# Building the sink values of a new sequence one operation per step, over six steps

## The chip, the cores and the metric
The kernel runs on one core of one Trainium2 chip. The metric is the device time of one execution in microseconds, taken as the median over several executions. The profile is one execution recorded by the hardware profiler; its times are microseconds from the first instruction of the core.

## The reference, cut to what matters
Windowed attention with a few "sink" keys that every query may see, and behind it a dense layer with a softplus in the middle:
```
B, H, S, D = 4, 8, 768, 64          n_sink, window = 4, 128
scores = (1/sqrt(D)) * q @ k.T
keep   = (pos_k < n_sink) | ((pos_q - pos_k >= 0) & (pos_q - pos_k < window))
a      = softmax(where(keep, scores, -1e9))
x      = (a @ v) with the heads side by side            # [B*S, 512]
h      = x @ w_in                                       # w_in  [512, 2048]
out    = (max(h, 0) + log1p(exp(-abs(h)))) @ w_out      # w_out [2048, 512]
```

## The kernel before, in words
**Tiles.** The 4 sequences of 768 positions are cut into chunks of 256 positions, three to a sequence and twelve in all (chunks 0 to 11). A chunk has 8 heads. Chunks 0, 3, 6 and 9 are the first of their sequence. Chunks 0 and 1 (`EXACT = 2`) use full-precision operands; from chunk 2 on every matmul operand is split into a rounded high part and a remainder, and the matmuls run over both.

**Steps.** The work is a software pipeline with one step per head: step i = 8k + h. The first 17 steps are written out by hand in a string (`START`). From step 17 on a loop (L630 to L641) runs the same list of parts in each step: first the letters `JjGL`, then those of `STEADY`. A letter is a stage of some head ahead of or behind step i: `L` and `G` load, `p` and `q` split the loaded tiles, `S` the score matmuls, `T` the softmax, `N` the normalisation, `W` transposes the weights of head i and masks them, `V` the matmul of weights and values for head i, `O` its output, and `U F P R D E` are the dense layer of the chunk before. Each engine executes its instructions in the order in which this list issues them, and waits for data through semaphores. SyncE (SP) issues the loads and the stores in the same order.

**What GpSimd (POOL) does in a steady step**, in this order: the masking of the transposed weights into the tile `pt` (`W`, four selects, L308 and L311), in odd steps the remainder of the value tile `vv` (`q`, L56), the copy `gh` of the dense layer (`P`, L52), in odd steps the remainder `xl` (`O`, L56), and two normalisations of `a` (`N`, L264).

**What TensorE (PE) does in a steady step** that bears on the change: stage `V` (`values`, L316) first multiplies the sink weights with the sink values, `x<-sk,vs` (L327), and then the tile `pt` with the value tile, `x<-pt,vv` (L333); the other matmuls of the step are those of `h` (L459), `acc` (L496 to L498), the scores (L230, L231) and the transposes.

**The sink values.** `vs` is a tile of 128 partitions for a group of four heads, two groups (g = 0 and 1) to a sequence. Its lower 64 partitions hold the values of the sink keys of the group, each in the partition rows of its own head and zero elsewhere (a product with the 0/1 tile `hmask`, `_place`, L159): the left half of the columns holds the high part, the right half the remainder. Its upper 64 partitions are zero (`_zero`, L60). A new sequence is prepared as follows (k is its first chunk):
- step 8k-2, at its head (letter `J`): the load `vsr` of the raw values (L137, a DMA of SP), then on POOL the rounded copy `vsh` (L151), the remainder written back into `vsr` (L152), the zeroing of `vs` of group 0 (L154) and the two `_place` of group 0;
- step 8k+1, at its head (letter `j`): the zeroing and the two `_place` of group 1.

Heads 0 to 3 read group 0 in stage `V` of steps 8k to 8k+3, heads 4 to 7 group 1 in steps 8k+4 to 8k+7. The tiles have one buffer each (`bufs=1`). In the steady loop this happens for k = 3, 6 and 9, around steps 24, 48 and 72. The same for sequence 0 happens once in exact form and once more for chunk 2, whose `J` and `j` stand at steps 14 and 17.

Of the kernel before, what the change touches and what calls it, by code (L numbers as in the profile page):

```python
# [11 lines left out]
F32 = mybir.dt.float32  # L12
F32R = mybir.dt.float32r
# [7 lines left out]
B, H, S, D = 4, 8, 768, 64  # L21
DM, DFF = 512, 2048
P = 128
# [4 lines left out]
CT = CH * P  # L28
# [8 lines left out]
BIG = 3.0e38  # L37
G = 4
ORDERED = {mybir.EngineType.PE, mybir.EngineType.SP}


class Ctx:
# [16 lines left out]
def _zero(nc, out, finite):  # L59
    nc.gpsimd.tensor_scalar(out, finite, 0.0, 0.0, ALU.mult, ALU.add)  # L60
# [62 lines left out]
class _Attention:  # L123
# [16 lines left out]
    def sinks(self, g):  # L140

        c, nc, b = self.c, self.c.nc, self.b
        raw = c.vsr[b]
        if self.exact:
            c.vs[b, g] = c.lp.tile([P, G, D], F32, tag=f"vsf{g}", name=f"vsf{g}", bufs=1)
            nc.gpsimd.memset(c.vs[b, g][:], 0.0)
            self._place(c.vs[b, g][:32], raw[:32, g : g + 1], 32)
            return
        if g == 0:
            c.vsh[b] = c.lp.tile([64, 2, D], F32R, tag="vsh", name=f"vsh{b}", bufs=1)  # L150
            nc.gpsimd.tensor_scalar(c.vsh[b][:], raw[:], 1.0, 0.0, ALU.mult, ALU.add)  # L151
            nc.gpsimd.tensor_tensor(raw[:], raw[:], c.vsh[b][:], ALU.subtract)  # L152
        c.vs[b, g] = c.lp.tile([P, G, P], F32R, tag=f"vs{g}", name=f"vs{b}_{g}", bufs=1)
        _zero(nc, c.vs[b, g][64:].rearrange("p (a e) d -> p a (e d)", a=2), c.sk[64:].bitcast(F32).unsqueeze(1).broadcast_to([64, 2, CT]))  # L154
        for src, o in ((c.vsh[b], 0), (raw, D)):
            self._place(c.vs[b, g][:64, :, o : o + D], src[:, g : g + 1], 64)

    def _place(self, out, src, rows):
        self.c.nc.gpsimd.tensor_tensor(  # L159
# [350 lines left out]
def _fast(c):  # L510
# [5 lines left out]
    n = c.nchunks  # L516
    att = [_Attention(c, k) for k in range(n)]
# [24 lines left out]
    def stage(kind):  # L542
        def run(i):
            if not todo[kind]:
                return
            o, e = todo[kind][0]
            before = "acdl"["acdl".index(kind) - 1]
            while kind != "a" and todo[before] and todo[before][0][0] <= o:
                stage(before)(i)
            home = _turn(c.WM, o)  # L550
            if kind == "a":
                while any(u is c.upper[c.turn] for u in c.top.values()):
                    stage("c")(i)
            elif kind == "c" and home == "p":
                while sum(_turn(c.WM, k) == "p" for k, _ in todo["l"] if k < o) > 1:
                    stage("l")(i)
            todo[kind].pop(0)
            if kind == "a":
                _weight_top(c, e, _turn(c.WT, o))
            elif kind == "c":  # L560
                _weight_f32(c, e, home)
            elif kind == "d":
                _weight_high(c, e, engine(c.WH, o))
            else:
                _weight_low(c, e, _turn(c.WL, o) if home == "s" else "V")

        return run
# [11 lines left out]
    def sinks(g):  # L579
        def run(i):  # L580
            k = (i - g * G) // H
            if (i - g * G) % H == 0 and k < n and (att[k].first or k == c.EXACT):
                if g == 0 and k:
                    att[k].load_sinks()
                att[k].sinks(g)

        return run

    parts = {
        "S": (call(att, "scores"), G),  # L590
# [15 lines left out]
        "G": (call(att, "load_v", 2), 2),  # L606
        "L": (call(att, "load"), G + 2),
        "J": (sinks(0), 2),
        "j": (sinks(1), G - 1),
        "w": (dma, 0),  # L610
        **{kind: (stage(kind), 0) for kind in "acdl"},
    }
# [183 lines left out]
def _kernel(tc, a, out):  # L796
# [7 lines left out]
    with ExitStack() as keep:  # L804
        c.const = keep.enter_context(tc.tile_pool(name="const", bufs=1))
        c.wp = keep.enter_context(tc.tile_pool(name="wp", bufs=1))
        c.w, c.raw, c.top, c.word = {}, {}, {}, {}
        c.ident = c.const.tile([P, P], F32, name="ident")
        c.stats = c.const.tile([P, B * H * NB], F32, name="stats")
        c.room = c.const.tile([P, 2, 4 * FP], F32, name="room")  # L810
        nc.gpsimd.memset(c.room[:], 1.0)
        c.sk = c.const.tile([P, CT], F32R, name="sk")
        ones = c.room[:].rearrange("p a b -> p (a b)").unsqueeze(1).broadcast_to([P, CT // 64, 64])
        _zero(nc, c.sk[:].rearrange("p (a b) -> p a b", b=64), ones)
        with ExitStack() as st:
            pool = lambda n, bufs: st.enter_context(tc.tile_pool(name=n, bufs=bufs))
            psum = lambda n, bufs: st.enter_context(tc.tile_pool(name=n, bufs=bufs, space=bass.MemoryType.PSUM))
            c.xp, c.mp, c.stg = pool("xp", 2), pool("mp", 2), pool("stg", 4)
            c.lp, c.ap, c.sp = pool("lp", 2), pool("ap", 2), pool("sp", 2)
            c.ps_acc, c.ps_h = psum("ps_acc", 1), psum("ps_h", 2)  # L820
            c.ps_s, c.ps_t, c.ps_x = psum("ps_s", 2), psum("ps_t", 1), psum("ps_x", 1)
            with tc.manual_schedule(engines=ORDERED):
                _fast(c)
        ok = nc.values_load(c.flag[:1, :1], min_val=0, max_val=1)
        with tc.If(ok < 1):
            _general(c)
# [8 lines left out]
Ctx.WT = "PAAVVVVAVAAVAAAVAAAAAAAAAAAPAAAV"  # L835
Ctx.WH = "VAPAAVAAAAVPPAAAAVVAVAAAAAVAVAAA"
Ctx.WL = "PPPPPPPVPPVPPVPPVPVPPPPVVPVVPVPV"
Ctx.STEADY = ("kWUqpKSFTRDVPONE", "SWTkpUKERDNFPqVO")
Ctx.START = """
S0 G4 T0 w w S1 j4 T1 J0 w L8 w w S3 S2 N0 N1 T2 W0 L10 w N2 S4 T3 N3 a w T4 k0 a c K0 a S5 c W1 w w  # L840
d S6 V0 O0 l d V1 w c l T5 N4 W2 T6 d w a S7 c O1 W3 l N5 G6 N6 a T7 c V2 N7 a d S8 k4 a O2 W4 w T8
# [62 lines left out]
```

## Time and profile before
| | |
|---|---|
| median of 3 runs | 740.09 us |
| lowest and highest run | 737.24 and 740.62 us |
| span of the profiled execution | 735.7 us, 13883 instructions |
| mean granted TensorE clock of that execution | 0.986 of full |
| busy: PE, DVE, ACT, POOL | 95%, 75%, 61%, 54% of the span |

The page of the profile gives the span of the profiled execution, from its first to its last instruction, and no other time of its own for it; the median of the runs lies 4.4 us above this span and the lowest run 1.5 us above it. A row of a timeline gives the start in us, the duration in us, the engine, the line, the operation, the output and input tiles with their shapes, how many instructions were merged, and in square brackets the idle time of the engine just before with the instruction that ended it. A row of the waits names who waited for whom, then the total in us, the number of times and the longest. A row of the table of windows gives the stretch, its length, the busy time and instruction count of PE, PEld (the weight loads), DVE, ACT and POOL, and then the granted clock, the DMA share and GB/s.

### The profile page before, as it was taken

The numbers are of one execution on the slowest core, as the hardware profiler recorded it, in microseconds if no ns is written. First come the engines' busy times: TensorE is split into PE (matmuls) and PEld (weight loads), VectorE is DVE, ScalarE is ACT, GpSimd is POOL, SyncE is SP. The second block draws the span as 40 slices with busy tenths as digits, with TensorE's granted clock in tenths as the row PEclk, the third lists the DMA queues.
The fourth block names the chain that finished last, engine by engine and source line by source line (L and its number), as shares of the span: only waits on it lengthen the run. The fifth ranks groups of instructions, "written<-read, shape, count | busy, mean of one in ns | idle before, by whom it ended". The sixth has DMA issues, their size and how long they took to land.

```text
span 735.7 us, 13883 instructions
## 1 busy us (share of the span) xinstructions
PE 699.7 (95%) x4489; PEld 624.8 (85%) x4489; DVE 552.6 (75%) x1608; ACT 446.1 (61%) x1098; POOL 400.7 (54%) x773
## 2 busy tenths in 40 slices
PE   4788899989999999998999999998999999999996
PEld 3567688979899999997899999997999999999995
DVE  5899997867877877876977887886887877754331
ACT  3577865655666666665666666665766756644331
POOL 4866476565555665665655655556655565553110
PEclk9899999999999999999999999999999999999999
DMA  8877611411321321321321322322222222100001
GB/s 291 310 255 235 187 40 48 126 46 44 98 67 49 105 61 54 93 63 42 92 74 49 95 69 57 95 60 61 62 74 77 83 61 76 58 13 0 30 1 35
DMA packets 40876, 63.22 MB, mean 86 GB/s; under 512 B 4634, under 2 KB 22362, under 8 KB 40794
## 3 DMA queue, kind: packets, MB, share of 16 engines
q1 hardware_dynamic: 36042, 45.47, 21.2%
q10 hardware_dynamic: 4752, 16.77, 6.5%
q8 instruction: 38, 0.62, 0.4%
q14 instruction: 44, 0.36, 0.2%
HBM read 55.93 MB, written 6.29 MB: 85 GB/s over the span
## 4 chain that ended last, share of the span: by engine, by line
PE 83%; DVE 6%; POOL 4%; ACT 3%; DMA 1%; issue 1%; ACTq 0%; SPq 0%; POOLq 0%; DVEq 0%
PE h L459 34%; PE acc L496 11%; PE acc L498 11%; PE acc L497 11%; PE x L333 6%; PE t L297 2%; PE s L230 2%; PE s L231 2%; PE x L327 2%; PE s L227 1%; ACT a L250 1%; POOL a L264 1%; DMA wo71r<-w 1%; POOL pt L308 1%; PE ts L281 1%
## 5 line engine op out<-in xcount | busy, mean ns | idle before, releaser
L459 PE MATMUL h<-xh,wi 128*128 128x256 f32 x1536 | 254.6, 289 | 0.0
L459 PEld LDWEIGHTS h<-xh,wi 128*128 128x128 f32 x1536 | 212.3, 192 | 1.2 <-issue 0.3
L459 PE MATMUL h<-xl,wi 128*128 128x256 f32 x768 | 154.9, 284 | 0.0
L496 PE MATMUL acc<-wo,gh 128*128 128x512 f32 x384 | 153.7, 400 | 0.0
L498 PE MATMUL acc<-wo,gl 128*128 128x512 f32 x384 | 151.7, 395 | 0.7 <-DVE gl L56 0.7
L497 PE MATMUL acc<-wo,gh 128*128 128x512 f32 x384 | 151.5, 395 | 0.0
L52 POOL TENSOR_SCALAR gh<-mt 128x512 fp32r<-128x512 f32 x91 | 56.5, 621 | 166.7 <-DVE mt L474 165.4
L466 ACT ACTIVATE mt<-h 128x512 f32<-128x512 f32 x96 | 57.2, 596 | 114.2 <-PE h L459 114.2
L459 PEld LDWEIGHTS h<-xl,wi 128*128 128x128 f32 x768 | 120.0, 192 | 0.0
L264 POOL TENSOR_SCALAR a<-a,rc 128x128 f32<-128x128 f32 x180 | 71.9, 411 | 87.1 <-DVE rc L257 78.8
L250 ACT ACTIVATE a<-a,stats 128x136 f32<-128x136 f32 x192 | 75.9, 396 | 39.1 <-DVE stats L249 39.0
L474 DVE SCALAR_TENSOR_TENSOR mt<-h,mt 128x512 f32<-128x512 f32 x96 | 65.9, 687 | 42.4 <-ACT mt L468 28.2
L498 PEld LDWEIGHTS acc<-wo,gl 128*128 128x128 f32 x384 | 72.8, 189 | 17.8 <-DVE gl L56 1.2
L496 PEld LDWEIGHTS acc<-wo,gh 128*128 128x128 f32 x384 | 72.8, 190 | 12.9 <-issue 0.4
L497 PEld LDWEIGHTS acc<-wo,gh 128*128 128x128 f32 x384 | 72.9, 190 | 9.3
L56 DVE TENSOR_TENSOR gl<-mt,gh 128x512 fp32r<-128x512 f32 x96 | 70.5, 734 | 4.4 <-POOL gh L52 4.0
L467 ACT ACTIVATE mt<-mt 128x512 f32<-128x512 f32 x96 | 60.8, 633 | 3.1
L468 ACT ACTIVATE mt<-mt 128x512 f32<-128x512 f32 x96 | 60.7, 633 | 3.0
L351 DVE TENSOR_TENSOR xt<-x,xt 64x256 f32<-64x256 f32 x80 | 33.2, 415 | 38.9 <-ACT xt L48 38.9
L243 DVE COPY_PREDICATED s<-diag,s 128x128 f32<-128x128 int32 x192 | 49.1, 289 | 15.4 <-PE s L231 11.9
L48 ACT CAST qkh<-qk 128x656 fp32r<-128x656 f32 x80 | 59.3, 741 | 0.4 <-DMA qk<-qk 0.4
L333 PE MATMUL x<-pt,vv 128*128 128x256 f32 (+1 forms) x216 | 48.7, 328 | 7.9 <-POOL pt L311 7.9
(183 smaller groups left out, 1234.9 us busy)
## 6 DMA issues: line engine op xcount, KB each, us to landing
qk<-qk SPq DMA_DIRECT2D x160, 164.0 KB, 3.0
vr<-v SPq DMA_DIRECT2D x32, 192.0 KB, 2.8
out<-o SPq DMA_DIRECT2D x24, 256.0 KB, 2.3
q<-q SPq DMA_DIRECT2D x8, 256.0 KB, 4.7
vr<-v SPq DMA_DIRECT2D x16, 128.0 KB, 2.1
k<-k SPq DMA_DIRECT2D x8, 200.0 KB, 4.9
wi00r<-w ACTq DMA_DIRECT2D x1, 511.8 KB
wi01r<-w ACTq DMA_DIRECT2D x1, 511.8 KB
```

The lines of the kernel that those rows point to most:

```text
L48: nc.scalar.copy(out, in_)
L56: (nc.vector if eng == "V" else nc.gpsimd).tensor_tensor(out, a, b, ALU.subtract)
L250: nc.scalar.activation(a, a, AF.Exp, bias=nm, scale=-1.0, accum_out=sm[:, j : j + 1])
L264: (nc.vector if eng == "V" else nc.gpsimd).tensor_scalar(a, a, rc[:, j : j + 1], 0.0, ALU.mult, ALU.add)
L333: nc.tensor.matmul(x[:, :, o], w, pt[:, :, m], start=False, stop=n == 2, skip_group_check=True)
L459: nc.tensor.matmul(h[:, j], wt, x, start=k == 0, stop=k >= len(prods) - 2, skip_group_check=True)
L467: nc.scalar.activation(t[:], t[:], AF.Exp, scale=-1.0)
L468: nc.scalar.activation(t[:], t[:], AF.Ln, bias=1.0)
L474: nc.vector.scalar_tensor_tensor(t[:], h[:], 0.0, t[:], ALU.max, ALU.add)
L496: nc.tensor.matmul(acc[:], gh[:, j, q], wh, start=f == 0, stop=False, skip_group_check=True)
L497: nc.tensor.matmul(acc[:], gh[:, j, q], wl, start=False, stop=False, skip_group_check=True)
L498: nc.tensor.matmul(acc[:], gl[:, j, q], wh, start=False, stop=f == 2 * FP - 1, skip_group_check=True)
```

## The change
The ten POOL instructions and the load that prepare a later sequence are dealt out to seven places, each at the end of a step (new letter `Y`, behind `V`, `O` and `N` and ahead of `E`). The zeroing is done for sequence 0 only: later sequences write into the same two `vs` tiles, whose upper 64 partitions stay as they are. Letters `J` and `j` remain for chunks 0 and 2 only.

- step 8k-6: the load `vsr`
- step 8k-4: the rounded copy `vsh`; step 8k-3: the remainder
- steps 8k-2 and 8k-1: one `_place` each for group 0
- steps 8k+1 and 8k+2: one `_place` each for group 1

```
+SINK_STEPS = {
+    -6: ("load_sinks",),
+    -4: ("sink_split", 0),
+    -3: ("sink_split", 1),
+    -2: ("sink_half", 0, 0),
+    -1: ("sink_half", 0, 1),
+    1: ("sink_half", 1, 0),
+    2: ("sink_half", 1, 1),
+}
...
         if g == 0:
+            self.sink_split(0)
+            self.sink_split(1)
+        for e in range(2):
+            self.sink_half(g, e)
+
+    def sink_split(self, e):
+        c, nc, b = self.c, self.c.nc, self.b
+        raw = c.vsr[b]
+        if e == 0:
             c.vsh[b] = c.lp.tile([64, 2, D], F32R, tag="vsh", name=f"vsh{b}", bufs=1)
             nc.gpsimd.tensor_scalar(c.vsh[b][:], raw[:], 1.0, 0.0, ALU.mult, ALU.add)
+        else:
             nc.gpsimd.tensor_tensor(raw[:], raw[:], c.vsh[b][:], ALU.subtract)
...
+    def sink_half(self, g, e):
+        c, nc, b = self.c, self.c.nc, self.b
+        if b == 0 and e == 0:
+            c.vs[b, g] = c.lp.tile([P, G, P], F32R, tag=f"vs{g}", name=f"vs{b}_{g}", bufs=1)
+            _zero(nc, c.vs[b, g][64:]...)
+        else:
+            c.vs[b, g] = c.vs[0, g]
+        src, o = ((c.vsh[b], 0), (c.vsr[b], D))[e]
+        self._place(c.vs[b, g][:64, :, o : o + D], src[:, g : g + 1], 64)
...
-            if (i - g * G) % H == 0 and k < n and (att[k].first or k == c.EXACT):
+            if (i - g * G) % H == 0 and k in (0, c.EXACT):
...
+    def next_sinks(i):
+        for k in range(c.EXACT + 1, n):
+            if att[k].first:
+                what, *args = SINK_STEPS.get(i - k * H, ("first",))
+                if what != "first":
+                    getattr(att[k], what)(*args)
...
+        "Y": (next_sinks, 0),
...
-Ctx.STEADY = ("kWUqpKSFTRDVPONE", "SWTkpUKERDNFPqVO")
+Ctx.STEADY = ("kWUqpKSFTRDVPONYE", "SWTkpUKERDNFPqVOY")
```

More of the change, by code (lines that the diff above doesn't have):

```diff
@@ L149, in sinks @@
         if g == 0:
+            self.sink_split(0)
[6 more added lines that the diff above has]
+        if e == 0:
             c.vsh[b] = c.lp.tile([64, 2, D], F32R, tag="vsh", name=f"vsh{b}", bufs=1)
             nc.gpsimd.tensor_scalar(c.vsh[b][:], raw[:], 1.0, 0.0, ALU.mult, ALU.add)
+        else:
             nc.gpsimd.tensor_tensor(raw[:], raw[:], c.vsh[b][:], ALU.subtract)
[L153 to L156, printed above, removed]
+    def sink_half(self, g, e):
+        c, nc, b = self.c, self.c.nc, self.b
+        if b == 0 and e == 0:
+            c.vs[b, g] = c.lp.tile([P, G, P], F32R, tag=f"vs{g}", name=f"vs{b}_{g}", bufs=1)
+            _zero(nc, c.vs[b, g][64:].rearrange("p (a e) d -> p a (e d)", a=2), c.sk[64:].bitcast(F32).unsqueeze(1).broadcast_to([64, 2, CT]))
+        else:
+            c.vs[b, g] = c.vs[0, g]
+        src, o = ((c.vsh[b], 0), (c.vsr[b], D))[e]
+        self._place(c.vs[b, g][:64, :, o : o + D], src[:, g : g + 1], 64)
     def _place(self, out, src, rows):
```

## The prediction
> **What bounds the kernel now.** I read the page first. Its lines on the span and on the busy engines:
> ```profile
> span 735.7 us, 13883 instructions
> ...
> PE 699.7 (95%) x4489; PEld 624.8 (85%) x4489; DVE 552.6 (75%) x1608; ACT 446.1 (61%) x1098; POOL 400.7 (54%) x773
> ```
> TensorE is busy for 95% of the span, so a change on POOL can pay only where POOL makes TensorE wait. The second view is therefore the waits of TensorE alone, from 135 us (behind the hand-written start) to the end:
> ```profile
> PE x L333 <- POOL pt L311: 7.9, 5, 2.4
> ```
> This is the only row of that answer: in 600 us TensorE waits five times, always in stage V, for the masked weights `pt` of POOL. The third view is the timeline of TensorE around these waits. I use the first instruction of stage V, `x<-sk,vs` (L327), as the mark of a step. The first two rows are steps 8k-2 and 8k-1 of chunk 5, which begins no sequence; then come the same two steps ahead of chunks 6, 9 and 3, which begin one:
> ```profile
> 275.64 0.28 PE L327 MATMUL x<-sk,vs 128*128 128x256 f32 x1
> 282.56 0.28 PE L327 MATMUL x<-sk,vs 128*128 128x256 f32 x1
> ...
> 331.56 0.28 PE L327 MATMUL x<-sk,vs 128*128 128x256 f32 x1
> 334.23 0.73 PE L333 MATMUL x<-pt,vv 128*128 128x256 f32 x3 [2.39 <-POOL pt L311]
> 341.17 0.28 PE L327 MATMUL x<-sk,vs 128*128 128x256 f32 x1
> ...
> 501.71 0.28 PE L327 MATMUL x<-sk,vs 128*128 128x256 f32 x1
> 511.30 0.28 PE L327 MATMUL x<-sk,vs 128*128 128x256 f32 x1
> ...
> 160.01 0.28 PE L327 MATMUL x<-sk,vs 128*128 128x256 f32 x1
> 171.04 0.28 PE L327 MATMUL x<-sk,vs 128*128 128x256 f32 x1
> ```
> Without a new sequence the interval is 6.92 us; with one it is 9.61, 9.59 and 11.03 us. The excess is 2.69, 2.67 and 4.11 us, together 9.47 us. The reader is to see that a wait shown as 2.39 us costs 2.69 us: the pipeline needs another 0.3 us to start again. The third view also says who is late, and POOL's timeline for the same moment says why (`a` ends step 8k-3, `pt` is the first work of step 8k-2):
> ```profile
> 328.22 0.93 POOL L264 TENSOR_SCALAR a<-a,rc 128x128 f32<-128x128 f32 x2
> 329.12 0.60 POOL L151 TENSOR_SCALAR vsh<-vsr 64x128 fp32r<-64x128 f32 x1
> 329.80 0.45 POOL L152 TENSOR_TENSOR vsr<-vsr,vsh 64x128 f32<-64x128 f32 x1
> 330.35 0.62 POOL L60 TENSOR_SCALAR vs<-sk 64x512 fp32r<-64x512 f32 x1
> 331.04 1.13 POOL L159 TENSOR_TENSOR vs<-vsh,hmask 64x256 fp32r<-64x256 f32 x1
> 332.14 0.60 POOL L159 TENSOR_TENSOR vs<-vsr,hmask 64x256 fp32r<-64x256 f32 x1
> 332.70 0.40 POOL L308 TENSOR_SCALAR_AFFINE_SELECT pt<-th 128x256 fp32r<-128x256 f32 x1
> ```
> Five sink operations hold `pt` back from 329.12 to 332.70, that is 3.58 us, of which TensorE could hide about 1.2.
>
> Why the first of the three costs more shows in the table of windows, where the granted clock is the column behind POOL:
> ```profile
> 160.00:171.00 11.00, 8.62 (x47) 7.45 (x46) 6.06 (x18) 4.30 (x12) 6.63 (x14) 0.84 0.06 19
> ...
> 331.60:341.20 9.60, 7.21 (x48) 6.36 (x47) 5.92 (x18) 4.32 (x12) 6.63 (x14) 1.00 0.07 19
> ...
> 173.00:735.00 562.00, 550.22 (x3622) 501.09 (x3620) 409.25 (x1189) 337.86 (x824) 293.15 (x587) 1.00 0.21 61
> ```
> Behind the stall at 160 us the clock was 0.84 over the interval, against 1.00 at the second and, over 562 us, afterwards. So 4.11 minus about 2.69, or 1.42 us, is a clock that fell after the pause.
>
> **Removing the block at step 8k-2.** Of the five operations only the remainder (330.35 - 329.80 = 0.55 us with its gap) still stands between `a` and the `pt` of this step, since it now closes step 8k-3. The stall goes if `pt` then comes in time, which the next rows decide. Gain: 9.47 us, 1.42 of it by the clock. [...] The trace speaks for the stall: the clock is down in the one stretch behind this pause and 1.00 over the 562 us of the last row.
>
> **Removing the block at step 8k+1.** It has no stall in its own step, yet one step later there is one in two of three cases. The rows: POOL's block, a subtraction of DVE beside it (chunk 6), the same subtraction at chunk 5, and the marks of steps 8k+2 and 8k+3 at chunks 6 and 9:
> ```profile
> 351.29 0.62 POOL L60 TENSOR_SCALAR vs<-sk 64x512 fp32r<-64x512 f32 x1
> 351.99 0.61 POOL L159 TENSOR_TENSOR vs<-vsh,hmask 64x256 fp32r<-64x256 f32 x1
> 353.12 0.40 POOL L308 TENSOR_SCALAR_AFFINE_SELECT pt<-th 128x256 fp32r<-128x256 f32 x1
> ...
> 353.19 2.19 DVE L56 TENSOR_TENSOR qkh<-qk,qkh 64x256 fp32r<-64x256 f32 x1
> ...
> 294.70 0.42 DVE L56 TENSOR_TENSOR qkh<-qk,qkh 64x256 fp32r<-64x256 f32 x1
> ...
> 361.95 0.28 PE L327 MATMUL x<-sk,vs 128*128 128x256 f32 x1
> 369.42 0.28 PE L327 MATMUL x<-sk,vs 128*128 128x256 f32 x1
> ...
> 532.08 0.28 PE L327 MATMUL x<-sk,vs 128*128 128x256 f32 x1
> 538.89 0.28 PE L327 MATMUL x<-sk,vs 128*128 128x256 f32 x1
> ```
> With the block, POOL runs without a gap from 351.29 on, and the subtraction of DVE beside it takes 2.19 us instead of 0.42. DVE's later work is late by that, POOL's next `gh` waits for it, the `pt` of step 8k+2 follows `gh`, and the interval is 7.47 us at chunk 6 against 6.81 at chunk 9. Chunk 3 looks like chunk 6, so the excess is twice 0.66, or 1.32 us. Without the block POOL has to wait for DVE at this point, as at chunk 5, and the subtraction should get through. Gain: 1.32 us, or nothing if DVE is still held up.
>
> **Adding one operation to six steps.** Each now stands between the `a` of its step and the `pt` of the next. What it may cost is what `pt` had in hand. The last select of the steps at chunk 5 (8k-3, 8k-2, 8k-1, 8k, 8k+2), and the marks that are not quoted yet (8k-3, 8k, 8k+2); the last row is step 8k+3 at chunk 9:
> ```profile
> 266.80 0.73 POOL L311 TENSOR_SCALAR_AFFINE_SELECT pt<-tl 128x256 fp32r<-128x256 f32 x1
> ...
> 274.57 0.40 POOL L311 TENSOR_SCALAR_AFFINE_SELECT pt<-tl 128x256 fp32r<-128x256 f32 x1
> ...
> 280.42 0.73 POOL L311 TENSOR_SCALAR_AFFINE_SELECT pt<-tl 128x256 fp32r<-128x256 f32 x1
> ...
> 288.00 0.41 POOL L311 TENSOR_SCALAR_AFFINE_SELECT pt<-tl 128x256 fp32r<-128x256 f32 x1
> ...
> 302.53 0.40 POOL L311 TENSOR_SCALAR_AFFINE_SELECT pt<-tl 128x256 fp32r<-128x256 f32 x1
> ...
> 268.70 0.28 PE L327 MATMUL x<-sk,vs 128*128 128x256 f32 x1
> ...
> 291.10 0.28 PE L327 MATMUL x<-sk,vs 128*128 128x256 f32 x1
> ...
> 303.60 0.28 PE L327 MATMUL x<-sk,vs 128*128 128x256 f32 x1
> ...
> 536.86 0.62 POOL L311 TENSOR_SCALAR_AFFINE_SELECT pt<-tl 128x128 fp32r<-128x128 f32 x1
> ```
> TensorE needs `pt` about 0.05 us behind the mark. So the cover is, step by step, and the operation that now uses it:
> - 8k-3: 268.75 - 267.53 = 1.22 us, against the copy `vsh`, 0.68 (329.12 to 329.80). It leaves 0.54.
> - 8k-2: 275.69 - 274.97 = 0.72, against the remainder, 0.55. It leaves 0.17.
> - 8k-1: 282.61 - 281.15 = 1.46, against a placing, 0.56 to 1.10 (the two placings above). It leaves at least 0.36.
> - 8k: 291.15 - 288.41 = 2.74, against a placing. Ample.
> - 8k+2: 303.65 - 302.93 = 0.72, against a placing. Between 0.16 in hand and 0.38 too late.
> - 8k+3: 538.94 - 537.48 = 1.46, against a placing. At least 0.36 in hand.
>
> Only step 8k+2 is in doubt. In hand it costs 0; too late it costs 0.38 and 0.3 for the restart, 0.68 for each sequence, 2.0 us in all. It sits nearer to the short value, since the same operation at this end of the kernel took 0.61 (351.99): I take 0.2 a sequence, 0.6 us. If the cover of a step were gone altogether, its operation would cost its whole 0.55 to 1.10 us.
>
> **Zeroing, load, reuse.** Six zeroings are dropped; both blocks that held them are already counted, so they add nothing. The load moves from step 8k-2 to 8k-6 on SP's queue, behind loads that run several steps ahead, and has two steps, some 14 us, until `vsh` needs it: 0. Writing into the old tile must wait until TensorE has read it. Group 0 was last read in step 8k-5 and is written from 8k-2 on, group 1 was last read in 8k-1 and is written from 8k+1 on, so no wait comes of it: 0.
>
> **Sum.** 9.47 + 1.32 - 0.6 = 10.2 us off the span of 735.7, which gives 725.5. With the 4.4 us by which the median of the runs lies above this span, it is 729.9, rounded to 730.0 us.
>
> **Rivals.**
> 1. DVE is still held up at 8k+1. There the 1.32 us stay, the third sequence gets its 0.66 as well, and the placing in front of `pt` at 8k+2 adds its 0.56 in full: 3 x 1.22 = 3.7 us are left of waits. The gain is 10.8 - 3.7 = 7.1 us, or 733.0 us; should step 8k-2 overrun too, some 0.5 us each, 734.5. For it: a POOL operation ahead of `pt` lengthens POOL's unbroken run, and 0.17 us in hand is little. Against it: the subtraction took 0.42 us at chunk 5. [...] The trace's 2.19 us is longer than any one select here.
> 2. The clock is not the stall's doing and falls anyway. Then 1.42 us less are gained: 731.4 us. [...]
> 3. Something else is just as late at step 8k-2 (the chain through ACT and DVE to `pt`), or the reused tile brings a wait after all. Then little changes: 738 to 740 us. Against it stand the 6.92 us of the steps at chunk 5, where all else is the same.
> 4. Slower: the six operations find no cover. They cost 0.68 + 0.55 + 1.10 + 3 x 0.56 = 4.0 us a sequence, 12.0 in all, and each stall its 0.3 us of restart, 18 times or 5.4. Against a gain of 10.8 that is 6.6 us slower, 746.7 us. It decides from the point where `pt` already ends behind the mark in these steps; the covers above (0.72 to 2.74 us) speak against it.
>
> **How the numbers follow.** My forecast has 0.60, rival 1 has 0.18, rival 2 has 0.10, rival 3 has 0.08 and rival 4 has 0.04. The forecast's own range is from 729.3 (no cost at 8k+2) to 731.3 (2.0 us there). The runs of before scatter by 3.4 us, their lowest 2.9 below the median, so I widen to 727.5 below; above, rivals 1 and 2 are taken in, up to 735.0. A measurement of this kernel can tell about 0.5%, or 3.7 us, from no change. Forecast and rivals 1 and 2 are faster by more: 0.88. Rival 3 is within: 0.08. Rival 4: 0.04.
>
> **What would show it.** In the profile of the changed kernel the marks of steps 8k-2 and 8k-1 should lie 6.9 us apart at chunks 3, 6 and 9, with no wait for `pt` there and a clock of 1.00 behind 135 us. The subtraction of DVE at 8k+1 should take 0.4 to 0.7 us, and the interval behind 8k+2 about 6.8 to 7.2. TensorE's waits from 135 us on should add up to under 1.5 us instead of 7.9. The prediction is wrong if an interval of 9 us remains, if many small waits for `pt` appear in steps 8k-3 to 8k+3, or if TensorE waits as long for another engine.

## The result and the profile after
| | before | after |
|---|---|---|
| median of 6 runs | 740.17 us | 734.26 us |
| lowest and highest | 737.24, 740.62 us | 732.61, 735.2 us |
| span of the profiled execution | 735.7 us | 733.0 us |

The ratio is 0.9923, with a 95% interval from 0.9907 to 0.9940: the median is 5.9 us lower, where 10.1 were forecast. The time lies inside the range, nearest to that of rival 1. The page of the changed kernel (its lines are numbered anew: L327 is L356, L333 is L362, L56 is L67):
```profile
span 733.0 us, 13874 instructions
...
PE 699.9 (95%) x4489; PEld 624.4 (85%) x4489; DVE 564.5 (77%) x1608; ACT 447.1 (61%) x1098; POOL 394.0 (54%) x767
```
POOL is busy 6.7 us less, but DVE 11.9 us more with the same 1608 instructions. That is the first hint: nothing was given to DVE, so some of its instructions must have become longer. The waits of TensorE from 135 us on, in us in total, times and the longest:
```profile
PE x L362 <- POOL pt L340: 2.6, 3, 0.9
PE ts L310 <- DVE sa L298: 2.6, 3, 0.9
```
The 7.9 us of before are gone, yet the six waits of 0.86 us are regular: one for POOL and one for DVE in each sequence. TensorE's timeline around chunk 6 (marks of steps 8k-2, 8k-1, 8k, 8k+2 and 8k+3, and the two waits):
```profile
330.56 0.28 PE L356 MATMUL x<-sk,vs 128*128 128x256 f32 x1
331.70 0.74 PE L362 MATMUL x<-pt,vv 128*128 128x256 f32 x3 [0.86 <-POOL pt L340]
338.62 0.28 PE L356 MATMUL x<-sk,vs 128*128 128x256 f32 x1
345.19 0.38 PE L310 MATMUL ts<-ident,sa 128*32 128x128 f32 x2 [0.86 <-DVE sa L298]
348.18 0.28 PE L356 MATMUL x<-sk,vs 128*128 128x256 f32 x1
360.42 0.28 PE L356 MATMUL x<-sk,vs 128*128 128x256 f32 x1
367.24 0.28 PE L356 MATMUL x<-sk,vs 128*128 128x256 f32 x1
```
Behind 8k-2 it is 8.06 us now instead of 9.61, with 6.92 as the undisturbed value; behind 8k+2 it is 6.82 instead of 7.47. But behind 8k-1 it is 9.56 us, where the kernel before had 8.53: a wait that did not exist. Chunks 3 and 9 show the same to 0.04 us. The table of windows, with the granted clock behind POOL's column:
```profile
160.00:171.00 11.00, 10.14 (x64) 8.83 (x63) 9.62 (x26) 6.92 (x18) 6.80 (x15) 1.00 0.17 46
...
135.00:720.00 585.00, 579.84 (x3832) 528.50 (x3831) 448.76 (x1271) 360.81 (x880) 310.03 (x626) 1.00 0.22 62
```
The clock stays at 1.00 from 135 to 720 us, through all six waits.

In sum, the eight steps from 8k-3 to 8k+5 took 60.03, 58.63 and 57.94 us at chunks 3, 6 and 9, and take 57.41, 57.44 and 57.43: 4.3 us less. The rest of the 5.9 us between the medians is not shown by these two traces. Their starts differ by 1.65 us in the other direction (the mark of step 16 stands at 119.54 before and 121.19 after); over all the traces of this study, whose start is the same code, this mark lies between 119.54 and 122.62.

So where does DVE lose the time? Its timeline around chunk 6, the three instructions that stand out:
```profile
321.08 2.33 DVE L67 TENSOR_TENSOR qkh<-qk,qkh 64x256 fp32r<-64x256 f32 x1
...
335.56 2.35 DVE L67 TENSOR_TENSOR qkh<-qk,qkh 64x256 fp32r<-64x256 f32 x1
...
343.62 1.43 DVE L298 TENSOR_TENSOR sa<-a,rc 128x64 f32<-128x64 f32 x1
```
The subtraction that takes 0.42 us in an ordinary step takes 2.33 in step 8k-3 and 2.35 in 8k-1, and the 0.23 us product `sa` takes 1.43 at the head of 8k. POOL's timeline beside the first of them, up to the late selects:
```profile
319.71 0.72 POOL L293 TENSOR_SCALAR a<-a,rc 128x128 f32<-128x128 f32 x2 [0.95 <-DVE rc L286]
320.40 0.29 POOL L172 TENSOR_SCALAR vsh<-vsr 64x128 fp32r<-64x128 f32 x1
320.66 0.40 POOL L337 TENSOR_SCALAR_AFFINE_SELECT pt<-th 128x256 fp32r<-128x256 f32 x1
321.01 0.40 POOL L340 TENSOR_SCALAR_AFFINE_SELECT pt<-th 128x256 fp32r<-128x256 f32 x1
...
322.11 1.01 POOL L67 TENSOR_TENSOR vv<-vr,vv 128x384 fp32r<-128x384 f32 x1
326.21 0.62 POOL L63 TENSOR_SCALAR gh<-mt 128x512 fp32r<-128x512 f32 x1 [3.09 <-DVE mt L503]
...
329.00 0.77 POOL L174 TENSOR_TENSOR vsr<-vsr,vsh 64x128 f32<-64x128 f32 x1
...
331.25 0.40 POOL L340 TENSOR_SCALAR_AFFINE_SELECT pt<-tl 128x256 fp32r<-128x256 f32 x1
```
The new copy `vsh` took only 0.29 us, less than forecast, and the selects behind it were in time. But POOL then runs without a gap until `vv` ends at 323.12, and DVE's subtraction, issued at 321.08, ends at 323.41, 0.29 us behind that. DVE is 1.9 us late, POOL waits 3.09 us for DVE's tile `mt` before it can make `gh`, everything behind `gh` slides, and the `pt` of step 8k-2 ends at 331.65, 1.09 us behind the mark at 330.56.

At 8k it is different. The hold from 335.56 on makes DVE late again, but `sa` starts only 0.41 us late: 5.00 us behind the mark of 8k-1, against 4.59 without any sink operation (e1 below). Then `sa` is held up itself, for 1.2 us. POOL beside it, the placing at the end of 8k-1 and the last select of 8k:
```profile
343.39 0.61 POOL L188 TENSOR_TENSOR vs<-vsr,hmask 64x256 fp32r<-64x256 f32 x1
...
344.92 0.29 POOL L340 TENSOR_SCALAR_AFFINE_SELECT pt<-tl 128x128 fp32r<-128x128 f32 x1
```
`sa` was issued 0.23 us into the placing and ended at 345.05, while the last select was still under way. Of the 1.60 us that it ends late against the mark, 1.03 show in the interval (9.56 - 8.53); TensorE hides the other 0.57, which is more than the 0.41 of the late start. So the wait at 8k needs the sink operation at the end of 8k-1, which e2 and e8 below bear out.

### The profile page after: what moved, and what is told of

It reads as the page before. It is cut to its first block, busy times and chain, and to the rows that moved or that the text cites. A ratio compares the mean times of both kernels' runs of the same rounds, so it can differ in the third digit from the quotient of the medians.

```text
span 733.0 us, 13874 instructions
## 1 busy us (share of the span) xinstructions
PE 699.9 (95%) x4489; PEld 624.4 (85%) x4489; DVE 564.5 (77%) x1608; ACT 447.1 (61%) x1098; POOL 394.0 (54%) x767
## 4 chain that ended last, share of the span: by engine, by line
PE 78%; DVE 12%; ACT 4%; POOL 3%; issue 1%; DMA 1%; ACTq 0%; SPq 0%; DVEq 0%; POOLq 0%
PE h L488 32%; PE acc L525 10%; PE acc L527 10%; PE acc L526 10%; PE x L362 5%; PE t L326 2%; PE s L259 2%; PE s L260 2%; DVE qkh L67 2%; PE x L356 2%; PE s L256 1%; ACT a L279 1%; DVE s L272 1%; DVE sa L298 1%; DMA wo71r<-w 1%
## 5 line engine op out<-in xcount | busy, mean ns | idle before, releaser
L67 DVE TENSOR_TENSOR gl<-mt,gh 128x512 fp32r<-128x512 f32 x96 | 69.8, 727 | 4.4 <-POOL gh L63 4.1
L67 DVE TENSOR_TENSOR qkh<-qk,qkh 64x256 fp32r<-64x256 f32 x80 | 53.7, 672 | 14.8 <-ACT qkh L59 9.4
```

The source lines that it names most:

```text
L67: (nc.vector if eng == "V" else nc.gpsimd).tensor_tensor(out, a, b, ALU.subtract)
```

## The experiments
Two theories were set against each other. The **hold**: a DVE instruction with two inputs in SBUF (the memory in which the kernel keeps `qk`, `qkh`, `a` and `rc`), issued while a POOL instruction is under way, waits until POOL's unbroken run of instructions is over, and the small operations ahead of the selects moved POOL's instruction boundaries so that DVE loses where it had won. The **queue**: POOL simply has too much work ahead of `pt`, and DVE's long subtraction is without weight. The intervals below are those of all three chunks, which agree to 0.05 us. Of e1, e2, e3, e6 and e7 there is one execution each (728.36, 730.2, 731.04, 739.63 and 733.53 us), so they are read by the intervals of their traces; ratios are to executions of the kernel before that were taken beside the run.

**Nothing at all (e1).** In `next_sinks` the operations are dropped and only the tiles' names are handed on, so this kernel and that of e2 leave out the sink values of sequences 1 to 3 and read those of sequence 0:
```
-                if what != "first":
-                    getattr(att[k], what)(*args)
+                if what == "load_sinks":
+                    for g in range(2):
+                        c.vs[att[k].b, g] = c.vs[0, g]
```


> This kernel leaves out the ten sink operations of sequences 1 to 3 altogether (they read the sink values of sequence 0), so it gives the most that any placing of them can gain. Both theories: the marks of stage V at chunks 3, 6 and 9 lie 6.9 us (8k-2), 8.5 us (8k-1) and 6.8 us (8k+2) apart, no wait for the weights or the sink weights there, the subtraction of DVE takes 0.4 to 0.7 us. That is 2.15 us a sequence or 6.4 us below the changed kernel, 10.8 us below the kernel before.

Measured: no wait of TensorE at all behind 135 us, marks 6.93, 8.53 and 6.82 us apart, the subtraction never above 0.8 us. TensorE's marks of 8k-2, 8k-1 and 8k, and `sa` of step 8k:
```profile
329.20 0.28 PE L356 MATMUL x<-sk,vs 128*128 128x256 f32 x1
336.13 0.28 PE L356 MATMUL x<-sk,vs 128*128 128x256 f32 x1
344.66 0.28 PE L356 MATMUL x<-sk,vs 128*128 128x256 f32 x1
...
340.72 0.24 DVE L298 TENSOR_TENSOR sa<-a,rc 128x64 f32<-128x64 f32 x1
```
The eight steps take 55.29 us, 10.7 us in all below the kernel before: that is the ceiling, and the gross gain of the prediction (10.8) was right. The description of the change and the expectation speak of ten POOL operations to a sequence; POOL has 773 instructions before, 767 after the change and 749 here, so it was eight before and is six after.

**Only a trace of an operation (e2).** The same, with a tiny operation (64x2) in the six places:
```
+                elif what != "first":
+                    _zero(c.nc, c.tiny[:], c.hmask[:, :2])
```


> This kernel leaves out the sink operations of sequences 1 to 3 and puts in each of the six places a POOL operation on two columns, some 0.1 to 0.2 us. Theory of the hold (DVE's subtraction with two inputs in SBUF, issued while a POOL instruction is under way, waits for the whole unbroken run of POOL; an operation ahead of the selects moves POOL's instruction boundaries against DVE): the subtraction is still held for 1.5 us or more in step 8k-3 or 8k-1, and an interval of 7.5 us or more remains. Theory of the queue (POOL has just too much work ahead of the masked weights, DVE's long subtraction is a side effect without weight): 0.2 us is far within the cover of 0.7 us or more, so all intervals are those without sink operations, 6.9, 8.5 and 6.8 us.

Measured, on POOL and on DVE in step 8k-3, and `sa` of step 8k:
```profile
319.12 0.18 POOL L71 TENSOR_SCALAR tiny<-hmask 64x2 f32<-64x2 f32 x1
...
319.63 0.40 POOL L341 TENSOR_SCALAR_AFFINE_SELECT pt<-th 128x256 fp32r<-128x256 f32 x1
...
320.73 1.01 POOL L67 TENSOR_TENSOR vv<-vr,vv 128x384 fp32r<-128x384 f32 x1
```
```profile
319.80 2.22 DVE L67 TENSOR_TENSOR qkh<-qk,qkh 64x256 fp32r<-64x256 f32 x1
...
341.15 1.27 DVE L299 TENSOR_TENSOR sa<-a,rc 128x64 f32<-128x64 f32 x1
```
An operation of 0.18 us, a quarter of the smallest cover (0.72), makes DVE lose 1.8 us, again until 0.28 us behind the end of POOL's run (322.02 against 321.74). The intervals are 7.24 to 7.27 us behind 8k-2 and 8.97 to 9.02 behind 8k-1, where e1 has 6.93 and 8.53. Behind 8k-1 the tiny operation in front of the selects of 8k does it: `sa` starts 4.60 us behind the mark (336.55), as early as in e1, and takes 1.27 us instead of 0.24. The queue falls: by it 0.18 us of work, far within the covers, changes no interval. The hold's expectation was met in the duration. In the intervals it was not: the 7.5 us or more that it asked for did not come behind 8k-2, and behind 8k-1 the undisturbed 8.53 is above 7.5 already, so the effect on TensorE was smaller than I wrote.

**The copy one step earlier (e3).**
```
-    -4: ("sink_split", 0),
+    -5: ("sink_split", 0),
```


> The rounded copy moves from step 8k-4 to 8k-5, all else as in the changed kernel. Theory of the hold: the subtraction in step 8k-3 takes 0.4 to 0.7 us again, the dense layer's copy is 1.4 us earlier, and the interval from 8k-2 to 8k-1 falls from 8.06 to 6.9 to 7.2 us (the remainder's 0.55 us fits into 0.72); the wait for the sink weights at 8k stays, 9.5 us. Theory of the queue: the remainder still stands ahead of the selects of 8k-2, so the wait of 0.86 us and the 8.06 us stay.

Measured: 6.92 us behind 8k-2, with the remainder still ahead of the selects there, and no wait for `pt`. Behind 8k-1 it is 9.83 us, 0.3 more than in the changed kernel. DVE in steps 8k-3 and 8k-1:
```profile
319.04 0.42 DVE L67 TENSOR_TENSOR qkh<-qk,qkh 64x256 fp32r<-64x256 f32 x1
...
332.67 2.35 DVE L67 TENSOR_TENSOR qkh<-qk,qkh 64x256 fp32r<-64x256 f32 x1
```
The wait at 8k-2 was made one step earlier, by the copy that my prediction had counted as covered.

**Zeroing once, alone (e5).** The kernel before, with this part of the change only:
```
+        if b == 0:
             c.vs[b, g] = c.lp.tile([P, G, P], F32R, tag=f"vs{g}", name=f"vs{b}_{g}", bufs=1)
             _zero(...)
+        else:
+            c.vs[b, g] = c.vs[0, g]
```


> The kernel before with one part of the change: the zeroing is done for sequence 0 alone, the blocks stay where they were. Both theories: the block at 8k-2 is 0.69 us shorter, so the wait there falls from 2.39 to 1.70 us and the interval from 9.6 to 8.9 us. Hold: whether the subtraction at 8k+1 is still held depends on where POOL's instruction boundaries fall, so 6.8 or 7.5 us behind 8k+2. If the clock falls only behind long pauses, the interval at chunk 3 is now 8.9 as well instead of 11.03, and the time is 2.1 to 4.5 us below the kernel before, 735 to 737 us.

Measured: 734.7 us, ratio 0.9918 (0.9894 to 0.9942). The wait is 1.49 us (expected 1.70), the interval 8.69 to 8.70 at all three chunks, the subtraction is not held, and behind 8k+2 it is 6.82. The windows at chunk 3:
```profile
160.00:171.00 11.00, 9.51 (x62) 8.40 (x61) 8.52 (x25) 5.89 (x14) 8.06 (x16) 1.00 0.12 33
```
The clock is 1.00 there. The eight steps take 57.05 us, 0.4 us less than with the whole change. **This part alone gains as much as the whole change.**

**Spreading alone (e6).** The changed kernel, every sequence zeroing its tiles again:
```
-        if b == 0 and e == 0:
+        if e == 0:
...
-            c.vs[b, g] = c.vs[0, g]
+            pass
```


> The changed kernel with the other part undone: every sequence zeroes its tiles again, ahead of the first placing of each group (ends of 8k-2 and 8k+1). Theory of the hold: the unbroken run in step 8k-1 is 0.7 us longer, so the subtraction there takes about 3.0 us instead of 2.35 and the interval behind 8k-1 grows from 9.54 to about 10.2 us; the 8.06 us behind 8k-2 stay. Theory of the queue: the selects of 8k-1 end 0.7 us later, still within their cover of 1.46 us less the placing's 0.57, so nothing changes at 8k-1 and 8k.

Measured in step 8k-1, POOL and DVE:
```profile
336.45 0.62 POOL L71 TENSOR_SCALAR vs<-sk 64x512 fp32r<-64x512 f32 x1
337.14 0.75 POOL L188 TENSOR_TENSOR vs<-vsh,hmask 64x256 fp32r<-64x256 f32 x1
...
339.31 0.74 POOL L67 TENSOR_TENSOR vv<-vr,vv 128x256 fp32r<-128x256 f32 x1
```
```profile
337.00 0.42 DVE L67 TENSOR_TENSOR qkh<-qk,qkh 64x256 fp32r<-64x256 f32 x1
337.46 3.02 DVE L67 TENSOR_TENSOR kl<-qk,qkh 128x400 fp32r<-128x400 f32 x1
```
The first subtraction slips through beside the gap from 337.07 to 337.14, and the next one, `kl`, is held for the 3.0 us that were expected. The interval behind 8k-1 is 10.04 to 10.07 us (expected 10.2), that behind 8k-2 stays at 8.05, and one of 7.88 us comes back behind 8k+2, which was not expected. The eight steps take 59.0 us, against 60.03, 58.63 and 57.94 in the kernel before: spreading alone is 0.4 and 1.1 us worse at chunks 6 and 9, and 1.0 better at chunk 3, where the clock had fallen.

**A shorter run beside the subtraction (e7).** In the changed kernel `q`, and with it the 1.0 us of `vv`, goes behind `gh` in every step but 8k, where it stands there already:
```
-Ctx.STEADY = ("kWUqpKSFTRDVPONYE", ...
+Ctx.STEADY = ("kWUpKSFTRDVPqONYE", ...
```


> The changed kernel with the letter q (the remainder of the value tile, 1.0 us on POOL in odd steps) moved from behind the selects to behind the dense layer's copy, in every step. Theory of the hold: POOL's unbroken run beside the subtraction of odd steps ends 0.7 to 1.0 us earlier, so a held subtraction at 8k-3 and 8k-1 takes about 1.3 to 1.6 us instead of 2.35, and the waits at 8k-2 and 8k shrink by as much or go. Theory of a fixed block or a rounding of the profile: it stays at 2.35 us.

Measured in steps 8k-3 and 8k-1, the last select of POOL's run and DVE's subtraction:
```profile
322.47 0.40 POOL L340 TENSOR_SCALAR_AFFINE_SELECT pt<-tl 128x256 fp32r<-128x256 f32 x1
...
336.78 0.58 POOL L340 TENSOR_SCALAR_AFFINE_SELECT pt<-tl 128x256 fp32r<-128x256 f32 x1
```
```profile
321.83 1.32 DVE L67 TENSOR_TENSOR qkh<-qk,qkh 64x256 fp32r<-64x256 f32 x1
...
335.83 1.28 DVE L67 TENSOR_TENSOR qkh<-qk,qkh 64x256 fp32r<-64x256 f32 x1
```
In 8k-3 the run ends at 322.87 and the subtraction at 323.15, 0.28 us behind it. It takes 1.32 us instead of 2.33, shorter by what was taken from the run; the waits shrink from 0.86 to 0.38 and 0.69 us. The length of this hold is the rest of POOL's run. In 8k-1 it is not: there the subtraction ends at 337.11, 0.25 us ahead of the end of the run, and the last select takes 0.58 us instead of 0.40, which goes with DVE getting in before it.

**The six operations behind the selects (e4, and with more executions e10; e9 is the changed kernel beside it).** The only edit to the changed kernel:
```
-Ctx.STEADY = ("kWUqpKSFTRDVPONYE", "SWTkpUKERDNFPqVOY")
+Ctx.STEADY = ("kWUqpKSFTRDVYPONE", "SWTkpUKERDNFYPqVO")
```


> The letter Y moves ahead of P, so each sink operation stands in the pause in which POOL waits for the dense layer's gate, behind the selects and no longer ahead of them. Theory of the hold: POOL's run beside the subtraction is that of a step without sinks, so it takes 0.4 to 0.7 us, the intervals are 6.9 to 7.1 and 8.5 to 8.7 us, and the time falls by 5 to 6.5 us against the changed kernel, to about 728 to 729 us. Theory of the queue: also no wait for the masked weights, but the wait for the sink weights at 8k, which it does not explain, stays: 3 us less, about 731 us. If the operations hold up DVE's remainder of the gate instead, the copy is late by up to 0.6 us and small waits come back.

> The changed kernel once more, timed on the same chip as the next two. Its steady steps repeat to 0.03 us, so the profile should again show 8.06 and 9.54 us in all three sequences and a time 5 to 6 us below the kernel before.

> The kernel with the six operations ahead of the dense layer's copy, with more rounds. The profile has no wait left, so 6.4 us less than the changed kernel, a ratio to the kernel before of 0.983 to 0.986.

Measured: 727.57 us, ratio 0.9846 (0.9802 to 0.9890), and again 728.68 us, 0.9846 (0.9829 to 0.9864); the changed kernel beside it 734.46 us, 0.9928 (0.9908 to 0.9947), with 8.07 and 9.53 to 9.54 us in all three sequences. In the traces of e4 and e10 TensorE waits for nobody behind 135 us, and the eight steps take 55.29 us, the ceiling. POOL in step 8k-3, with an operation in the pause ahead of `gh`, and DVE's subtraction beside it:
```profile
319.51 0.65 POOL L337 TENSOR_SCALAR_AFFINE_SELECT pt<-tl 128x256 fp32r<-128x256 f32 x1
...
320.83 1.01 POOL L67 TENSOR_TENSOR vv<-vr,vv 128x384 fp32r<-128x384 f32 x1
321.80 0.90 POOL L174 TENSOR_TENSOR vsr<-vsr,vsh 64x128 f32<-64x128 f32 x1
323.17 0.62 POOL L63 TENSOR_SCALAR gh<-mt 128x512 fp32r<-128x512 f32 x1 [0.46 <-DVE mt L503]
```
```profile
319.47 0.42 DVE L67 TENSOR_TENSOR qkh<-qk,qkh 64x256 fp32r<-64x256 f32 x1
```
The subtraction gets in ahead of the select of 319.51, as in a step without sinks. The remainder takes 0.90 us here and still leaves a pause of 0.46 in front of `gh`.

**The undivided blocks in the same place (e8, and with more executions e11).** The kernel before, zeroing and all, with two letters moved:
```
-                for part in "JjGL" + c.STEADY[i % H == 0]:
+                for part in "GL" + c.STEADY[i % H == 0]:
-Ctx.STEADY = ("kWUqpKSFTRDVPONE", "SWTkpUKERDNFPqVO")
+Ctx.STEADY = ("kWUqpKSFTRDVJjPONE", "SWTkpUKERDNFJjPqVO")
```


> The kernel before with its two whole blocks, zeroing included, moved from the head of steps 8k-2 and 8k+1 to the place ahead of the dense layer's copy of the same step. Theory of the hold: the place decides and not the spreading; POOL's runs beside the subtraction are those without sinks, the block of 3.6 us takes the pause of about 2 us and makes the copy some 1.6 us late, the next selects by up to 0.8 us of a cover of 1.46, so the interval behind 8k-2 is 6.9 to 7.3 us and the time 727 to 730 us. Theory of the queue: 3.6 us of work in one piece still delay the selects of 8k-1 beyond their cover, and a wait of 1 us or more appears at 8k-1.

> The kernel before with its whole blocks ahead of the dense layer's copy, with more rounds. It also has no wait left, so no difference from the kernel with the six spread operations that the measurement can tell.

Measured: 727.37 us, ratio 0.9814 (0.9787 to 0.9841), and again 727.29 us, 0.9833 (0.9810 to 0.9857). No wait of TensorE behind 135 us; 55.29 us for the eight steps. POOL's block in step 8k-2 and what follows, DVE's subtraction in 8k-1 and `sa` of 8k:
```profile
328.10 0.29 POOL L151 TENSOR_SCALAR vsh<-vsr 64x128 fp32r<-64x128 f32 x1
...
330.61 0.61 POOL L159 TENSOR_TENSOR vs<-vsr,hmask 64x256 fp32r<-64x256 f32 x1
331.19 0.61 POOL L52 TENSOR_SCALAR gh<-mt 128x512 fp32r<-128x512 f32 x1
...
333.92 0.73 POOL L56 TENSOR_TENSOR vv<-vr,vv 128x256 fp32r<-128x256 f32 x1
```
```profile
332.98 1.95 DVE L56 TENSOR_TENSOR qkh<-qk,qkh 64x256 fp32r<-64x256 f32 x1
...
340.65 0.24 DVE L269 TENSOR_TENSOR sa<-a,rc 128x64 f32<-128x64 f32 x1
```
One part of the expectation failed: POOL's run beside the subtraction is not that of a step without sinks. `gh` follows the block without a pause, POOL then runs on until 334.65, and the subtraction takes 1.95 us, to 334.93. Here that costs nothing: no sink operation stands ahead of the selects of 8k, `sa` takes its 0.24 us, and the interval behind 8k-1 is 8.53. So neither the spreading nor the saved zeroings were needed for the full gain: the two undivided blocks of before, a few places further down POOL's queue, are as good as the best of the other versions that were run.

## Why the prediction was right or wrong
**What bounds the kernel, and the gross gain: right.** 9.47 + 1.32 = 10.8 us were named as the price of the two blocks; with the operations left out, 10.7 us go.

**The clock: right as far as it was tested.** The 1.42 us at chunk 3 are gone: with pauses of 0.86 us (changed kernel) and 1.49 us (e5) the clock is 1.00 at that place, and the mean granted clock of every other kernel's executions in this study is 0.986 to 0.993 (one at 0.986, the others at 0.988 or more), that of the kernel before 0.978 to 0.986. Rival 2 is out. In the kernel before the clock fell behind a pause of 2.38 us at chunk 3 (0.84 over 160 to 171 us), and not behind those of 2.39 and 2.38 us at chunks 6 and 9: they lie in the 562 us at 1.00, so the windows speak for the prediction's reading in one pause of three. No run isolated the pause from the rest of the kernel, so that it caused the fall is supported and not proven.

**The step at 8k+1: right.** The interval behind 8k+2 fell from 7.47 to 6.82 us. In the changed kernel the subtraction of the step behind it, 8k+2, still takes 1.80 us, without a wait of TensorE.

**The covers: wrong, and this is the step that failed.** "8k-3: ... It leaves 0.54" and "8k: ... Ample" compared each operation with the slack of the next selects. For the selects of the same step that was correct. But it took the other engine's times for fixed. The operation at the end of 8k-4 was within its cover and still shifted POOL against DVE, so that the subtraction of DVE lost 1.9 us, and the wait came one step later. The one at the end of 8k-2 did the same in step 8k-1, and the one at the end of 8k-1, which had the ample cover of 2.74 us, held up `sa`: the wait came at 8k, for another engine. For 8k+2, the only doubtful step, the forecast was 0.6 us; it cost nothing. Instead the term that was put at 0.6 us measured 6.4: twice about 1.1 us in each of three sequences (8.06 - 6.92 and 9.54 - 8.53). By the prediction's own signs this speaks against its mechanism: TensorE's waits add up to 5.2 us instead of under 1.5, and half of them are for DVE.

**Rival 1 had the mechanism and the wrong place.** It priced a DVE hold at 8k+1 and 733.0 us; the hold came at 8k-3, 8k-1 and 8k. That the time fell between its figures of 733.0 and 734.5 us, and so into the range that was widened for it, is luck: it left 3.7 us of waits standing at other steps, where 6.4 us came at these. Its sign was in the quoted rows: 2.19 us against 0.42 was taken as a property of the block and not as a warning for every operation put ahead of the selects.

**The time outside the span** was taken as 4.4 us. The runs show 1.7 to 2.0 between an execution's time and its own span; so the profiled execution of the kernel before, with 735.7, took about 737.4 and was among the shortest. The difference of the two kernels is not touched by it.

**Left open:** what decides whether DVE gets in, and when. In the rows here it lost when it was issued 0.07 to 0.17 us after a select began (321.08 against 321.01, 319.80 against 319.63) or 0.23 us after a placing began (343.62 against 343.39), and won when 0.04 us were left to the next (e4, above: 319.47 against the select of 319.51, which then took 0.65 us instead of 0.40). At chunk 9 of the kernel before it was issued 0.04 us into a select and got in behind that one, with 0.72 us. Why the others did not get in at the next boundary, and some got in ahead of the run's last select, was not tried.

## What to carry to other kernels
Before an operation is put into the order of an off-path engine, look at which instructions of another engine become longer beside it and not only at the slack of its own next result: in e2 an operation of 0.18 us cost another engine 1.8 us. Put such work where its engine pauses anyway, behind the result that others wait for; here the place was worth 6 us and the division into six steps, ahead of the selects, nothing. And when a change has two parts, run each alone: the one that looked minor carried the gain.

## What the runs showed of the hardware that was not expected
The DVE operations that were held here, `qkh`, `kl` (e6) and `sa`, have two SBUF inputs, and they did not wait for one POOL instruction but for several in a row. Of `tl<-t,th`, whose `t` is not in SBUF, none was held: in the changed kernel all 77 from 135 us on took 0.41 to 0.43 us, that of 335.11 under the placing of 334.88 too, while `qkh` took 0.42 to 2.36. In four cases with both rows quoted `qkh` waited for the rest of the unbroken run and ended 0.28 to 0.29 us behind its end, with durations from 1.32 to 2.33 us instead of 0.42 (323.41 behind 323.12; 322.02 behind 321.74; 323.15 behind 322.87; 334.93 behind 334.65). It is not always the whole run: `sa` in the changed kernel (343.62) and the second subtraction of e7 (335.83) ended 0.16 and 0.25 us ahead of its end, without waiting for the last select. The reverse also shows: where DVE gets in first, the select lasts 0.65 us (e4) instead of 0.40.
